# A first MLP product in seven block products instead of eight: w1's combinations kept in DRAM and fetched through a ring

## The chip, the cores and the metric

The kernel runs on one core of a Trainium2 chip. The metric is the device time of one execution in microseconds (us); the times given are medians of several runs. Lower is better.

## What is computed

The reference is one transformer-like block on x of 2048 positions by 512 channels, with a condition vector c that makes six modulation vectors. The first half is a spectral filter (a two-dimensional real FFT, a product with weights, the inverse FFT), the second half a dense MLP with the Mish activation:

```python
mod = (silu(c) @ w_mod).reshape(...)          # sa, ca, ga, sb, cb, gb
h = layernorm(x) * (1 + ca) + sa
x = x + ga * irfft2(rfft2(h) * (w_r + 1j * w_i))
h = layernorm(x) * (1 + cb) + sb
act = mish(h @ w1 + b1)                       # w1: 512 x 1376
x = x + gb * (act @ w2)                       # w2: 1376 x 512
```

Everything is float32. The change concerns `h @ w1`, and what has to be prepared for it.

## The kernel before

The x tile stays on the chip as 16 row blocks of 128 positions. The spectral half has three stages; the last of them, called p3 here, runs over the 16 row blocks in steps s = 0 to 16: `p3_col` (L707, L708) multiplies on TensorE into a bank of tag A, ScalarE copies the bank out (L710), `p3_row` (L717) multiplies the copy into a bank of tag B, and VectorE adds that to x (L720). `norm_sums` (L122, L123) then makes the row block's mean and variance for the second layer norm, and `norm_scale` (L127, L135, L147) turns these into scales.

The MLP works on eight blocks b of 256 positions (NB = 8) and on six groups t of features (NT = 6): t = 1 to 5 are pairs of feature tiles of 128, t = 0 is the last tile of 96. Float32 precision comes from splitting each operand into a high part (rounded to the fp32r format) and a low part (the rest), and adding three of the four products: high x high, high x low, low x high.

For one block, the channel dimension lies in four tiles k of 128. `transpose_in` (L686) and `split_in` (L694 to L699) bring a block's h into the tile h2, high and low parts beside each other, so that one matmul with w1's high part has 512 columns (L796) and one with w1's low part 256 (L798). `up` does four and four of them for each feature tile. `front` evicts: ScalarE moves the low half with the bias (L806), VectorE adds the high half (L807). `back` applies Mish (L813) and forms four sums of quarter tiles (L823) for the second product; `halves` splits these into high and low (L758, L759); `down` (L849, and L841 for t = 0) is the second product, which has seven block products over halves of positions, features and channels already. In the last block, t = 3, 4, 5 and 0 are done plainly by `last_down` (L862, L865). `gather`, `chain` and `residual` (L872 to L896) combine the seven results and add them to x, on VectorE.

w1 is loaded in twelve pieces during p3 (`load_w1`), copied to a high part on ScalarE (`split_w1`, L661) and subtracted to a low part on GpSimd (L662); both parts then stay on the chip. w2's pieces are loaded, summed on GpSimd (`sum_w2`, L755) and split (L758, L759) in p3 and in the first two blocks; gating and plain splits for the last block come late (L778). `mod_column` (L115) makes modulation sums on VectorE.

All engines run their own instructions in program order, and that order is written out by hand: a loop over s for p3, then a loop over the 48 items (b, t), each of which calls `up(s)`, `front(s)`, `halves(s - 1)`, `back(s)` and `down(s - LAG)` with LAG = 2, so that TensorE alternates one item's first product with the second product of the item two before.

## Time and profile before

| what | value |
|---|---|
| median of 3 runs | 382.56 us (381.71 to 382.67) |
| span of the profiled execution, first to last instruction | 380.1 us |
| busy: TensorE, its weight loads, VectorE, ScalarE, GpSimd | 373.7, 340.0, 300.2, 250.5, 99.1 us |
| data moved | 36.49 MB read from and 4.20 MB written to HBM |

The profiled execution has a span, which leaves out what lies before its first and after its last instruction; no time of its own is given beside that, and the median of the runs is 2.46 us above it. Engines are named PE (TensorE matmuls), PEld (its weight loads), DVE (VectorE), ACT (ScalarE), POOL (GpSimd) and SP (the queue that issues most transfers). A row such as "252.09 2.52 PE bank L849 x21" has the start and length in us, the engine, the tile written, the line of the kernel and the number of instructions. In a group row, the figure after the bar is busy time in us, then the mean length of one instruction in ns, then the engine's idle time before the group and what ended it.

### The profile page before, as it was taken

Reading aid. Unit: us, or ns where it says so; the run is one execution under the profiler, and the core shown is the slowest. Engines: PE = TensorE matmul, PEld = TensorE weight load, DVE = VectorE, ACT = ScalarE, POOL = GpSimd, SP = SyncE. Lnnn points to the kernel's source line nnn. Section 1 sums busy time; section 2 is a strip of 40 time slices with the busy share of each in tenths; the row PEclk is TensorE's granted clock in tenths of the full one; section 3 lists DMA queues with packets and bytes.
Section 4 is the critical chain, followed back from the end, with each engine's and each line's share of the span. In section 5 each row is a group of like instructions: output and inputs, shape, how many; then the busy total and the mean of one; then the engine's idle time right before and its main releaser. Section 6 shows DMA issues by size and latency. Waiting matters only on the chain.

```text
span 380.1 us, 7142 instructions
## 1 busy us (share of the span) xinstructions
PE 373.7 (98%) x2612; PEld 340.0 (89%) x2612; DVE 300.2 (79%) x688; ACT 250.5 (66%) x532; POOL 99.1 (26%) x134
## 2 busy tenths in 40 slices
PE   8999999998999999999999999999999999999996
PEld 8999967778999989998998998998998999899985
DVE  2898968886989989989749758757865976887994
ACT  1798789995497558865844845845765674685751
POOL 0588747883664611300000000000000010017000
PEclk9999999999999999999999999999999999999999
DMA  7999997776454221111000100100100200222011
GB/s 235 380 354 344 362 359 237 252 231 212 128 140 143 77 85 58 56 30 55 3 0 2 55 2 0 58 0 3 55 2 0 78 0 2 75 67 82 2 55 55
DMA packets 21746, 41.14 MB, mean 108 GB/s; under 512 B 4016, under 2 KB 7184, under 8 KB 21456
## 3 DMA queue, kind: packets, MB, share of 16 engines
q1 hardware_dynamic: 19552, 33.75, 26.3%
q10 hardware_dynamic: 2160, 6.95, 6.2%
q8 instruction: 20, 0.33, 0.3%
q14 instruction: 14, 0.11, 0.1%
HBM read 36.49 MB, written 4.20 MB: 107 GB/s over the span
## 4 chain that ended last, share of the span: by engine, by line
PE 93%; DVE 3%; ACT 1%; DMA 1%; issue 0%; SPq 0%; ACTq 0%
PE bank L849 24%; PE bank L796 21%; PE bank L798 10%; PE bank L707 4%; PE bank L717 4%; PE bank L708 4%; PE bank L498 4%; PE bank L208 4%; PE bank L547 3%; PE bank L253 3%; PE bank L841 2%; PE bank L862 2%; PE bank L478 2%; PE bank L686 2%; PE bank L255 1%; PE bank L254 1%
## 5 line engine op out<-in xcount | busy, mean ns | idle before, releaser
L806 ACT ACTIVATE buf<-bank,b1n 128x256 f32<-128x256 f32 (+1 forms) x88 | 40.8, 471 | 66.8 <-PE bank L798 64.2
L807 DVE TENSOR_TENSOR buf<-buf,bank 128x256 f32<-128x256 f32 (+1 forms) x88 | 35.4, 417 | 37.3 <-ACT buf L806 37.2
L759 DVE TENSOR_TENSOR al<-buf,ah 128x512 fp32r<-128x512 f32 (+2 forms) x85 | 52.9, 645 | 0.9 <-ACT ah L758 0.9
L778 POOL TENSOR_TENSOR buf<-buf,modr 128x512 f32<-128x512 f32 (+1 forms) x3 | 4.0, 1322 | 182.8 <-DMA buf<-in_B_w_dram 175.6
L796 PE MATMUL bank<-h2e,w1h 128*128 128x512 f32 (+1 forms) x176 | 48.4, 397 | 0.0
L796 PE MATMUL bank<-h2o,w1h 128*128 128x512 f32 (+1 forms) x176 | 48.3, 396 | 0.0
L758 ACT CAST ah<-buf 128x512 fp32r<-128x512 f32 (+2 forms) x85 | 43.0, 548 | 1.4 <-DVE buf L823 1.1
L823 DVE TENSOR_TENSOR buf<-buf 128x128 f32<-128x128 f32 x148 | 40.8, 317 | 3.5 <-ACT buf L813 2.2
L813 ACT ACTIVATE buf<-buf 128x512 f32<-128x512 f32 (+1 forms) x48 | 28.6, 596 | 14.8 <-DVE buf L807 14.7
L849 PE MATMUL bank<-w2a,ah 128*128 128x256 f32 x161 | 34.9, 286 | 0.0
L796 PEld LDWEIGHTS bank<-h2e,w1h 128*128 128x128 f32 (+1 forms) x176 | 30.1, 187 | 4.5
L796 PEld LDWEIGHTS bank<-h2o,w1h 128*128 128x128 f32 (+1 forms) x176 | 30.1, 187 | 4.4
L849 PE MATMUL bank<-w2b,ah 128*128 128x256 f32 x147 | 31.8, 283 | 0.0
L798 PEld LDWEIGHTS bank<-h2o,w1l 128*128 128x128 f32 (+1 forms) x176 | 26.7, 185 | 4.2
L798 PEld LDWEIGHTS bank<-h2e,w1l 128*128 128x128 f32 (+1 forms) x176 | 26.7, 185 | 4.1
L798 PE MATMUL bank<-h2o,w1l 128*128 128x256 f32 (+1 forms) x176 | 27.8, 280 | 0.0
L798 PE MATMUL bank<-h2e,w1l 128*128 128x256 f32 (+1 forms) x176 | 27.8, 279 | 0.0
L849 PEld LDWEIGHTS bank<-w2a,ah 128*128 128x128 f32 x161 | 26.7, 191 | 0.0
L707 PE MATMUL bank<-kc,d 128*128 128x128 f32 x128 | 24.8, 276 | 0.5 <-ACT d L391 0.5
L708 PE MATMUL bank<-kc,d 128*128 128x128 f32 x128 | 24.7, 275 | 0.0
L849 PEld LDWEIGHTS bank<-w2b,ah 128*128 128x128 f32 x147 | 24.6, 191 | 0.0
L122 DVE BATCH_NORM_STATS2 st<-x 128x6 f32<-128x512 f32 x32 | 22.0, 689 | 0.4
(228 smaller groups left out, 981.1 us busy)
## 6 DMA issues: line engine op xcount, KB each, us to landing
buf<-in_B_w_dram SPq DMA_DIRECT2D x20, 256.0 KB, 3.0
x<-in_A_x_dram SPq DMA_DIRECT2D x16, 256.0 KB, 4.9
xring<-in_x_t_dram SPq DMA_DIRECT2D x16, 256.0 KB, 4.7
out_dram<-x SPq DMA_DIRECT2D x7, 512.0 KB, 2.6
buf<-in_w_mod_dram SPq DMA_DIRECT2D x9, 256.0 KB, 3.1
mraw<-in_km_dram SPq DMA_DIRECT2D x16, 128.0 KB, 4.7
wqa<-in_w_q_dram SPq DMA_DIRECT2D x4, 512.0 KB, 6.8
wqb<-in_w_q_dram SPq DMA_DIRECT2D x4, 512.0 KB, 7.2
```

The costliest lines, as they stand in the source:

```text
L122: nc.vector.bn_stats(t, x[:, n, :])
L707: nc.tensor.matmul(o, dj[:, 0:128], kc[0][:, n, :], start=True, stop=False)
L708: nc.tensor.matmul(o, dj[:, 64:192], kc[1][:, n, :], start=False, stop=True)
L758: nc.scalar.copy(h, r)
L759: nc.vector.tensor_tensor(l, r, plain(h), op=ALU.subtract)
L796: nc.tensor.matmul(ps, w1h[:, k, fs], h[:, k], start=(k == 0), stop=False)
L798: nc.tensor.matmul(ps[:, 0:256], w1l[:, k, fs], h[:, k, 0], start=False, stop=(k == 3))
L806: nc.scalar.activation(o, ps[:, 256:], AF.Identity, bias=b1n[:rows, f:f + 1])
L807: nc.vector.tensor_tensor(o, o, ps[:, 0:256], op=ALU.add)
L813: nc.scalar.activation(o, o, AF.Mish)
L823: nc.vector.tensor_tensor(o, p, q, op=op)
L849: nc.tensor.matmul(o, a[p][:, e], w2[t][q][:, r], start=(own and half == 0 and t == 1 and i == 0), stop=(end and i == 2 and (n, half) != ( ...
```

## The change

The first product is done over pairs: i counts four pairs of neighbouring blocks (s0 = 2i, s1 = 2i + 1), t = 1 to 5 the pairs of feature tiles, and the 512 channels are two halves. In each (i, t), w1's part is a 2 x 2 arrangement A11, A12, A21, A22 (features by channels) and h a 2 x 2 arrangement B11, B12, B21, B22 (channels by positions). The eight products of the parts become seven, by sums of parts (Winograd's form of Strassen's scheme): S1 = A21 + A22, S2 = S1 - A11, S3 = A11 - A21, S4 = A12 - S2; T1 = B12 - B11, T2 = B22 - T1, T3 = B22 - B12, T4 = B21 - T2. Each of the seven products has six matmuls of 256 columns: two channel tiles, three terms of high and low parts.

- The operands of w1 (three parts and four sums for each t, 256 KB each with high and low parts) are made once, written to DRAM (`keep_w1`), and in later pairs of blocks fetched (`fetch_w1`) into a ring of eight slots. Those of t = 2, 3 and 1 are made in p3, those of t = 4 and 5 during the first pair of blocks. The sums (`sum_w1`) are formed on GpSimd; the low part is a subtraction on VectorE for A11, A12 and A22 and on GpSimd for the sums.
- h is scaled into raw buffers (`scale_in`), T1 to T4 are formed on GpSimd (`sum_in`), and all eight arrangements are split by ScalarE and VectorE (`split_in`).
- The products of one (i, t) accumulate in one bank of tag A (two halves) and half a bank of tag D. The half named x[0:256] takes products 1, 6, 7 and 4 in turn; `evict` reads it after each with ScalarE. VectorE adds after products 2, 7 and 3.
- The single tile t = 0 is done without the scheme, in matmuls of 256 columns (`up_single`), and its second product is also cut to 256 columns.
- The residual's products and additions move from VectorE to GpSimd, in pieces of 512.
- The loop over items is gone. Every call gets a key, and the calls are issued in the order of their keys: one key is one of the seven products, and between two of them two pieces of three matmuls of the second product are issued. In the first pair of blocks only block 0's second products run beside the first products; from then on two blocks' run for each pair, and the last block's run after all first products.
- The scratch memory for descriptors is cut from 8192 to 1024 bytes.

The core of the diff:

```diff
-LAG = 2
+PRODUCTS = {1: ("A11", "B11"), 2: ("A12", "B21"), 3: ("S4", "B22"), 4: ("A22", "T4"), 5: ("S1", "T1"),
+            6: ("S2", "T2"), 7: ("S3", "T3")}
...
-    w1h = pm.tile([P, 4, F], F32R, name="w1h")
-    w1l = pm.tile([P, 4, F], F32R, name="w1l")
...
+    kept = {(t, a): dram.tile([P, 512], F32, name=f"w1_{t}_{a}") for t in range(1, NT) for a, _ in PRODUCTS.values()}
...
+    def space(t, a, k):
+        if (t, a) in ring:
+            return
+        w = act.tile([P, 7, P], F32R, name=("ah", "al")[k % 2]).rearrange("p e s -> p (e s)")
+        ring[t, a] = w[:, 0:512].rearrange("p (i k f) -> p i k f", i=2, k=2)
+
+    def slot_w1(key):
+        ring[key] = pm.tile([P, 2, 2, P], F32R, name="wr", tag="wr", bufs=8)
+
+    def fetch_w1(t, a):
+        slot_w1((t, a))
+        nc.sync.dma_start(plain(ring[t, a].rearrange("p i k f -> p (i k f)")), kept[t, a])
+
+    def sum_w1(t, a):
+        p, q, op = {"S1": ("A21", "A22", ALU.add), "S2": ("S1", "A11", ALU.subtract),
+                    "S3": ("A11", "A21", ALU.subtract), "S4": ("A12", "S2", ALU.subtract)}[a]
...
+        nc.gpsimd.tensor_tensor(src[t, a], src[t, p], src[t, q], op=op)
+
+    def split_w1(t, a):
+        w = ring[t, a]
+        nc.scalar.copy(w[:, 0], src[t, a])
+        eng = nc.vector if a[0] == "A" else nc.gpsimd
+        eng.tensor_tensor(w[:, 1], src[t, a], plain(w[:, 0]), op=ALU.subtract)
+
+    def keep_w1(t, a):
+        w = ring[t, a] if t > 3 or t == 1 and (t, a) in near else ring.pop((t, a))
+        nc.sync.dma_start(kept[t, a], plain(w.rearrange("p i k f -> p (i k f)")))
...
+    def sum_in(b, dst=None):
+        p, q = {"T1": ("B12", "B11"), "T2": ("B22", "T1"), "T3": ("B22", "B12"), "T4": ("B21", "T2")}[b]
...
+        nc.gpsimd.tensor_tensor(raws[b], p, q, op=ALU.subtract)
...
-            for k in range(4):
-                nc.tensor.matmul(ps, w1h[:, k, fs], h[:, k], start=(k == 0), stop=False)
-            for k in range(4):
-                nc.tensor.matmul(ps[:, 0:256], w1l[:, k, fs], h[:, k, 0], start=False, stop=(k == 3))
...
+    def up(i, t, j):
+        a, b = PRODUCTS[j]
+        w, h = ring.pop((t, a)), slots[b]
+        o = region(i, t, j)
+        n = 0
+        for p, q in TERMS:
+            for k in range(2):
+                nc.tensor.matmul(o, w[:, p, k, :], h[:, q, k, :], start=(j in (1, 5) and n == 0), stop=(n == 5),
+                                 skip_group_check=True)
+                n += 1
...
+        if j == 1:
+            identity(hold(s0, t)[:, 0:256], ps, f)
+        if j == 6:
+            identity(hold(s1, t)[:, 0:256], ps, f)
+        if j == 2:
+            o = raw[s0, t][:, 0:256]
+            nc.vector.tensor_tensor(o, o, ps, op=ALU.add)
+        if j == 7:
+            o = raw[s1, t][:, 256:]
+            identity(o, ps, f + 1)
+            nc.vector.tensor_tensor(o, o, ups[i, t, "z"][:, 0:256], op=ALU.add)
+        if j == 4:
+            nc.scalar.activation(raw[s0, t][:, 256:], ps, AF.Mish, bias=b1n[:, f + 1:f + 2])
+            o = raw[s0, t][:, 0:256]
+            nc.scalar.activation(o, o, AF.Mish)
+        if j == 3:
+            o = raw[s1, t][:, 0:256]
+            nc.vector.tensor_tensor(o, o, ps, op=ALU.add)
...
-        nc.vector.tensor_tensor(rows, rows, gbr.unsqueeze(1).to_broadcast([P, 2, D]), op=ALU.mult)
+        for i, r in enumerate((r0, r1)):
+            xb = x[:, 2 * b + i, :]
+            nc.gpsimd.tensor_tensor(r, r, gbr, op=ALU.mult)
+            nc.gpsimd.tensor_tensor(xb, xb, r, op=ALU.add)
...
+    def plan_w1(plan, t, load, key, step, at):
+        k = 7 * (t - 2)
+        plan.at(load, load_w1, t, at)
+        for i, a in enumerate(("A11", "S1", "A12", "S2", "A22", "S4", "S3")):
+            now = key + step * i
+            plan.at(now, space, t, a, k + i)
+            if a[0] == "S":
+                plan.at(now + 0.01, sum_w1, t, a)
+            late = now + 0.02 if a[0] == "A" else now + 3.4 * step
+            plan.at(late, split_w1, t, a)
+            plan.at(late + 0.55 * step, keep_w1, t, a)
...
+    plan_w1(plan, 2, 0.7, 2.1, 0.5, 0)
+    plan_w1(plan, 3, 2.5, 5.7, 0.5, 2)
...
+    plan_w1(plan, 1, 6.5, 9.3, 0.5, 0)
...
+    for b, s, dst in (("T1", 12, "B11"), ("T2", 12, None), ("T3", 13, None), ("T4", 13, "B21")):
+        plan.at(s + 0.5, sum_in, b, dst)
+    for b, s in (("B11", 11), ("B21", 12), ("T2", 14), ("T1", 14.5), ("T3", 15), ("T4", 16)):
+        plan.at(s + 0.4, split_in, b)
...
+            units += [(i, t, 1)] + [prev + (j,) for j in (4, 3)] + [(i, t, j) for j in (6, 2, 5, 7)]
...
+        if i == 0 and t > 3:
+            plan.at(k - 7.9, slot_w1, (t, a))
+            plan.at(k - (7.5 if t == 4 else 4.7), split_w1, t, a)
+            plan.at(k - 3, keep_w1, t, a)
+        elif k >= 8:
+            plan.at(k - 7.9, fetch_w1, t, a)
...
+            plan.at(key - 3.2, sums, b, t)
+            lead = 1.9 if t == 4 else 2.4
+            plan.at(key - lead, halves, b, t, 0)
+            plan.at(key - lead + 0.7, halves, b, t, 1)
...
+            for c in range(n):
+                plan.at(key + 0.5 * c, down, b, t, c)
```

532 lines of the change are left out of this document (301 added, 231 removed).

## The prediction

> **What bounds the kernel now.** I read the page's head first, then the windows by stage, then the chain of waits that ended last, and last single rows. The page gives the span, the busy time of each engine, and the chain that ended last by engine:
>
> ```profile
> span 380.1 us, 7142 instructions
> PE 373.7 (98%) x2612; PEld 340.0 (89%) x2612; DVE 300.2 (79%) x688; ACT 250.5 (66%) x532; POOL 99.1 (26%) x134
> PE 93%; DVE 3%; ACT 1%; DMA 1%; issue 0%; SPq 0%; ACTq 0%
> ```
>
> TensorE is the bound on average; whether it is where the change works is for the windows to say (a stretch in us and its length; busy us and instructions of PE, PEld, DVE, ACT and POOL; granted clock, DMA share, GB/s):
>
> ```profile
> 92.00:136.00 44.00, 44.00 (x388) 43.58 (x388) 38.95 (x78) 27.05 (x55) 23.78 (x24) 1.00 0.42 121
> 136.00:172.00 36.00, 35.92 (x239) 32.46 (x238) 33.72 (x80) 26.68 (x55) 6.79 (x8) 1.00 0.21 60
> 172.00:232.50 60.50, 60.50 (x415) 55.85 (x414) 43.21 (x104) 37.19 (x77) 0.00 (x0) 1.00 0.05 18
> ```
>
> The first row is the last stage of the spectral part (p3), in which the MLP's weights are prepared; the second is the MLP's start, the third two of its blocks in the steady state. TensorE has no gap in any of them, at full granted clock. In the steady state VectorE is 71% busy, ScalarE 61%, GpSimd idle and DMA at 5%: there is room for what the change adds. In p3 VectorE is at 89% and GpSimd at 54%, and then VectorE is at 94%: little room. So the gain is read from the third row, the danger from the first two.
>
> **What TensorE saves.** The chain gives the issue price of each shape (start, us, line, matmuls):
>
> ```profile
> 171.88 1.38 PE bank L841 x6
> 252.09 2.52 PE bank L849 x21
> 254.61 0.93 PE bank L796 x4
> 255.54 0.47 PE bank L798 x4
> 256.01 0.94 PE bank L796 x4
> ```
>
> L796 is the 512-column product with w1's high part, L798 the 256-column one with its low part: a feature tile of one block costs 0.93 + 0.47 = 1.40 us, two tiles of two blocks 5.60 us. L849 is the second product, whose matmuls are 256 columns wide, as all the new ones are: 2.52 / 21 = 0.12 us. The change does seven products of six matmuls, 42 x 0.12 = 5.04 us: 0.56 us less for each of 20 pairs (five pairs of tiles, four of blocks), 11.2 us. By L798's 0.47 / 4 = 0.1175 us it would be 5.60 - 4.94 = 0.66 us, 13.3 us in all. I take 0.12, since the new groups of six alternate with groups of three of L849's kind. The Trainium skill ("TensorE: Matmul & The Clock Gate", section "Wait — 56ns, not 53.3ns?") has a warm matmul start every N / 2.4 GHz + 2.5 ns, so 109 ns and 216 ns; this trace has 117.5 to 120 ns and 232 ns, and by the page's figures the estimate would be 12.2 us.
>
> The number of weight loads goes from 32 to 42 per pair. Their row (ns min/median/max, first and last start):
>
> ```profile
> L849 PEld LDWEIGHTS bank<-w2a,ah x161: 187/192/192, 151.7 to 362.3; 128*128 128x128 f32 x161
> ```
>
> A load of 192 ns stands before every 0.12 us matmul of L849 and is already in its interval, so I add nothing. The pairs would break even at 5.60 / 42 = 0.133 us for a matmul.
>
> Two pieces get dearer. The second product of the single 96-row tile goes from six wide matmuls (L841, 1.38 us) to twelve narrow ones, 1.44 us: 7 x 0.06 = 0.4 us. Its first product becomes twelve narrow ones, 1.44 for 1.41 us: 0.2 us. TensorE's own time falls by 11.2 - 0.6 = 10.6 us. Transposes stay, and blocks 0 to 7 keep the other matmuls of the second product.
>
> **What the change puts on VectorE and GpSimd.** Prices without company are from the steady state, where GpSimd is idle (busy us, mean ns):
>
> ```profile
> L823 DVE TENSOR_TENSOR buf<-buf 128x128 f32<-128x128 f32 x40 | 9.8, 287 | 1.1 <-ACT buf L813 0.7
> L807 DVE TENSOR_TENSOR buf<-buf,bank 128x256 f32<-128x256 f32 x20 | 8.2, 418 | 10.6 <-ACT buf L806 10.6
> L759 DVE TENSOR_TENSOR al<-buf,ah 128x512 fp32r<-128x512 f32 x10 | 6.9, 691 | 0.0
> L759 DVE TENSOR_TENSOR al<-buf,ah 128x384 fp32r<-128x384 f32 x10 | 5.6, 557 | 0.0
> ```
>
> Beside GpSimd the same operation is longer. From p3, groups and then single starts:
>
> ```profile
> L699 DVE TENSOR_TENSOR h2e<-buf,h2e 128x512 fp32r<-128x512 f32 x2 | 2.2, 1102 | 0.0
> L759 DVE TENSOR_TENSOR w2a<-buf,w2a 128x512 fp32r<-128x512 f32 x1 | 1.8, 1766 | 0.0
> L759 DVE TENSOR_TENSOR w2a<-buf,w2hi 128x512 fp32r<-128x512 f32 x1 | 1.8, 1761 | 0.0
> L759 DVE TENSOR_TENSOR w<-buf,w 128x512 fp32r<-128x512 f32 x1 | 1.2, 1218 | 0.0
> L759 DVE TENSOR_TENSOR w2a<-buf,w2a 128x256 fp32r<-128x256 f32 x1 | 0.4, 406 | 0.0
> L759 DVE TENSOR_TENSOR w2a<-modr,w2a 128x1024 fp32r<-128x1024 f32 x1 | 1.2, 1193 | 0.0
> L115 DVE SCALAR_TENSOR_TENSOR buf<-buf,bank 128x512 f32<-128x512 f32 x3 | 2.0, 672 | 1.4 <-DMA buf<-in_w_mod_dram 1.4
> L135 DVE SCALAR_TENSOR_TENSOR ve<-ve,rstd 128x2 f32<-128x2 f32 x2 | 1.6, 818 | 0.1
> L135 DVE SCALAR_TENSOR_TENSOR ve<-ve,rstd 128x4 f32<-128x4 f32 x2 | 0.3, 161 | 0.1
> L720 DVE TENSOR_TENSOR x<-x,bank 128x512 f32<-128x512 f32 x16 | 10.8, 675 | 2.4 <-PE bank L717 2.1
> ```
>
> ```profile
> 110.01 0.73 POOL L755 TENSOR_TENSOR modr<-buf 128x256 f32<-128x256 f32 x1
> 117.57 2.09 DVE L759 TENSOR_TENSOR w2a<-buf,w2a 128x256 fp32r<-128x256 f32 x2
> 117.70 1.42 POOL L662 TENSOR_TENSOR w1l<-buf,w1h 128x512 fp32r<-128x512 f32 x1 [2.13 <-ACT w1h L661]
> 122.83 1.28 POOL L662 TENSOR_TENSOR w1l<-buf,w1h 128x512 fp32r<-128x512 f32 x1 [1.76 <-ACT w1h L661]
> ```
>
> The pair at 117.57 needs about 0.41 + 0.69 us alone, and took 2.09, because its second half did not end before GpSimd's operation had. Operations of VectorE that read PSUM (L720) are not stretched. The five stretched subtractions lost (1766 + 1761 + 1218 - 3 x 691) + 2 x (1102 - 691) ns = 3.5 us, and the two of L135 at 818 ns against 161 another 1.3 us: some 5 us of p3's 38.95.
>
> In p3 the change replaces GpSimd's twelve low parts of w1 by 12 sums and 12 low parts of combinations (24 x 0.73 = 17.5 us), keeps 12 sums for w2 (8.8 us), and adds four sums of h (4 x 1.28 = 5.1 us) and the single tile's low part, about 1 us: 32.4 us against 23.78. VectorE gets nine low parts of w1 (9 x 0.41 = 3.7 us) and six splits of h in place of two (4 x 0.69 = 2.8 us). If the stretch grows with the number of its SBUF operations (13 more beside some 28, a factor of 1.4) and with GpSimd's time (32.4 / 23.78, again 1.4), 5 us becomes about 10 us, and VectorE has 38.95 + 6.5 + 5 = 50.5 us to do in 44. How late may it be before TensorE waits?
>
> ```profile
> 93.72 1.06 PE L717 MATMUL bank<-kiv,buf 128*128 128x128 f32 x8
> 94.61 0.39 PE L707 MATMUL bank<-kc,d 128*128 128x128 f32 x2
> 96.40 1.06 PE L717 MATMUL bank<-kiv,buf 128*128 128x128 f32 x8
> ```
>
> A step is 2.68 us, and L717's products go to two banks, so an addition (L720) may end up to 5.36 - 1.06 = 4.3 us after its products; it takes 0.68, so 3.6 us of lateness cost nothing. That leaves 50.5 - 44 - 3.6 = 2.9 us. The bounds: nothing, if TensorE's first MLP units (which need only B11 and w1's first combination) are reached with VectorE late, as it may be there; and, if VectorE and GpSimd never work beside each other on SBUF, 32.4 us of GpSimd and 16 us of VectorE (3.7, six splits at 0.69, the w2 splits' 5.7 from 406, 691 and 1193 ns, 16 small ones at 0.16) in the 13 steps that have them, 48.4 - 34.8 = 13.6, less 3.6: 10 us.
>
> ScalarE's queue has its own hazard there. w1's combinations of the later tiles are written into four slots that are read by the transfer to DRAM, and for two of them a tile, twice, the reading transfer is issued only a fraction of a step before the next write. Transfers of 256 KB land after 3.0 us:
>
> ```profile
> buf<-in_B_w_dram SPq DMA_DIRECT2D x20, 256.0 KB, 3.0
> ```
>
> The waiting copy holds up L710's eviction behind it, for which TensorE waits once it is over 1.2 us late (a step of 2.68 less the 0.89 us between the starts of L717 and the next column product, less 0.59 for the copy): 0 to 1.4 us each, four times, 0 to 5.6 us. It passes while VectorE is late anyway, and I take 1 us beyond the 2.9: p3 costs 3.9 us, between 0 and 10.
>
> In the first pair of blocks, evictions (15 x 0.42), sums and splits of one block's activations (5 x (9.8 + 6.9 + 5.6) / 10 + 0.4), w1's last splits (6 x 0.41), w2's (2 x 2.3 and 1.9), eight splits of h (8 x 0.69), four gate sums (4 x 0.75 with their read), the block's end (2 x 0.69 + 2 x 0.42) and small ones (0.6) make some 38 us of VectorE for some 43 us of TensorE (35 groups of 0.72, the single tile's 2.9 and one block's second product, 5 x 2.52 + 1.44, are 42.1; the transposes come on top), with 29 us of GpSimd beside it (24 x 0.73 for w1 and w2, 5.1 for the sums of h, 2 x 0.73 + 4 x 1.28 for the residual). By the rate of p3 that stretches VectorE by 5 to 8 us: just full. I take 1 us, between 0 and 7.
>
> In the steady state, a pair of blocks has 5 evictions by VectorE fewer (2.1 us) and both residuals moved to GpSimd, against four more splits of h (2.8 us); GpSimd gets about 18 us of 57. VectorE has room, and waits of at most 1.28 us are covered by parts issued two to three keys ahead (a key, one product of 0.72 us and two groups of 0.36, is 1.44 us). I take 0.1 us for each of three pairs, between 0 and 4 us in all.
>
> The ring: 35 fetches of 256 KB a pair of blocks, each issued on SP about eight products ahead, some 10 us, against 3.0 us to land. The stores behind them on SP wait for a slot at most, and nobody waits for these. At 9 MB in 57 us that is 157 GB/s, and the DMA share of 5% has the room. I cost it at nothing; without that lead each fetch would cost up to 3 us.
>
> The sum against the profiled execution: 380.1 - 10.6 + 3.9 + 1 + 0.3 = 374.7 us of span; the median of the runs, 382.56, lies 2.46 us above the span, so 377.2 us, and I say 377. A difference of 0.3%, 1.1 us, is about what a measurement here can tell from none.
>
> **Rivals.**
>
> All is hidden: TensorE stays without a gap, 382.56 - 10.6 = 372 us, or 370 by 0.1175. For it: the third window. Against it: VectorE at 94% after p3.
>
> VectorE and GpSimd become the bound until the second pair of blocks. For it: the stretched rows, and that both queues get more just there. It decides from the point where the last sum of h ends after p3's last product, since VectorE's queue then stands at the split of that sum with p3's last additions behind it. Price: 10 us in p3; in the first pair 29 us of GpSimd and 26 of VectorE's SBUF operations (the sums and splits above) in 43, less the 6.6 us residual that may slip, 5.4; and 1 us in each later pair: 382.56 - 10.6 + 10 + 5.4 + 3 = 390 us. The Trainium skill ("SBUF — State Buffer", section "SBUF: two separate sides") states it as a rule: a VectorE operation with two SBUF inputs and a GpSimd operation that reads SBUF exclude each other. By that rule the trace agrees at 117.57. Against it as the outcome: work in both queues is only due at its user.
>
> Halves of a bank: one 256-column region takes products 1, 6, 7 and 4 in turn, and each waits until ScalarE has read the one before. Between 7 and 4 lies one product and two or three groups of L849, 1.4 us; early in the first pair one product, 0.72 us. The eviction:
>
> ```profile
> L806 ACT ACTIVATE buf<-bank,b1n 128x256 f32<-128x256 f32 x20 | 9.4, 472 | 15.9 <-PE bank L798 15.9
> ```
>
> 0.47 us fits, unless ScalarE's queue stands at a copy that waits for VectorE. With a quarter of a microsecond for each of 20 pairs' tight waits it gives 377 + 5 = 382 us, no change.
>
> The change could also not save what it says, if a narrow matmul of the new order took over 0.133 us: at 0.14 it adds 42 x 0.14 - 5.60 = 0.28 us to each of 20 pairs, and with the other costs it is 382.56 + 5.6 + 0.6 + 5.2 = 394 us. The 21 in a row of L849 speak against it.
>
> **How the numbers follow.** Forecast (374 to 381) 0.45; all hidden 0.15; the shared bound 0.28; narrow matmuls too dear 0.02; halves of a bank 0.10, half of it no change and half slower. So faster 0.60, the same 0.05, slower 0.35. The range goes from 370.5, the hidden case, to 391, past the 390 of the second rival. The forecast's own range is 374 to 381.
>
> **What would show it.** Right: steady windows with TensorE full and a pair of blocks in some 57.7 us for 60.5; gaps of a few us at p3's end, put down to VectorE's additions (L720's successor) or ScalarE's copies; rows of the new products at 0.12 us. Wrong: a matmul interval over 0.13 us; gaps of 10 us or more in p3 and after with GpSimd full; waits of TensorE on ScalarE's evictions all along the steady state; or products that wait for a fetch.

## The result: 442.4 us, 15.6% slower

The changed kernel took 442.44 us (median; the kernel before beside it 382.58 us): a ratio of 1.156, 95% interval 1.152 to 1.160. The forecast was 377, the range 370.5 to 391, and the likeliest sign was the wrong one. The profiled execution took 443.01 us, with a span of 441.0.

First the page of the changed kernel: its span, the engines' busy time, the granted clock in 40 slices, and the chain that ended last by engine.

```profile
span 441.0 us, 8229 instructions
PE 392.6 (89%) x2886; PEld 368.3 (84%) x2886; DVE 333.1 (76%) x659; ACT 255.9 (58%) x560; POOL 203.1 (46%) x227
...
PEclk9999999999998878996989999988999999999969
...
PE 50%; DVE 33%; ACT 7%; DMA 4%; issue 4%; POOL 1%; SPq 1%; DVEq 0%; ACTq 0%; POOLq 0%
```

Before, TensorE held 93% of the chain and VectorE 3%. Now VectorE holds a third of it, although it is busy for no larger share of the span than before (76% for 79%): it is not full, it is late at particular places. And the row of granted clocks, all nines before, has sixes, sevens and eights from the thirteenth slice on.

The same windows by stage (stretch and length; busy us and instructions of PE, PEld, DVE, ACT, POOL; clock, DMA share, GB/s): p3, the first pair of blocks, the next pair, the end.

```profile
92.00:142.00 50.00, 45.02 (x388) 44.00 (x386) 44.92 (x81) 33.00 (x74) 35.26 (x41) 0.98 0.63 212
142.00:218.00 76.00, 60.36 (x407) 57.68 (x406) 50.05 (x103) 43.65 (x95) 26.69 (x29) 0.86 0.57 181
218.00:285.00 67.00, 62.17 (x496) 61.00 (x495) 49.40 (x95) 38.09 (x81) 20.66 (x16) 0.97 0.52 157
...
411.00:441.00 30.00, 19.32 (x105) 16.19 (x104) 23.14 (x28) 7.57 (x15) 16.60 (x13) 0.87 0.10 36
```

In the first pair nobody is full: TensorE 79%, VectorE 66%, ScalarE 57%, GpSimd 35%. What TensorE waited for (us in total, times, longest):

```profile
PE bank L940 <- DVE al L792: 16.5, 13, 3.7
PE bank L845 <- DVE even L862: 8.7, 4, 3.5
PE bank L845 <- DVE scb L862: 5.4, 2, 4.2
PE bank L754 <- DVE x L757: 2.7, 1, 2.7
```

L940 is the second product, which waits for the low parts of the activations (`halves`, L792). L845 is a first product that waits for VectorE's addition after product 2 (`evict`, L862), because that frees its half of a bank. No row names a fetch of the ring.

For a balance I took from both traces the time from each matmul's start to the next, less what is usual for its shape (the 20th percentile). Excess over 0.3 us at once is a gap; the rest is a slowed matmul, nearly all of it at half clock.

| stage (us of the changed kernel) | gaps | slowed | gaps and slowed before |
|---|---|---|---|
| p3, 92 to 142 | 5.6 | 2.2 | 0.4 |
| first pair, 142 to 218 | 17.3 | 10.6 | 0.9 |
| 218 to 411, the other pairs | 16.3 | 10.1 | 2.4 |
| end, 411 to 441 | 8.3 | 3.4 | 0.2 |
| sum | 47.5 | 26.3 | 3.9 |

That is 69.9 us more; the matmuls' usual intervals sum to 271.9 us for 280.8, so 8.9 us less. The difference, 61.0 us, is the change of the span (60.9). TensorE's saving is there; nearly eight times as much is lost beside it. The split is good to about 2 us: with the 20th percentile of each shape over the whole span as the usual interval, the saving comes to 7.1 us and the loss to 68.1.

Where the steady loss comes from shows in VectorE's, GpSimd's and TensorE's own rows of one place (start, length in us):

```profile
286.99 3.59 DVE L910 TENSOR_TENSOR buf<-buf 128x128 f32<-128x128 f32 x4
290.50 3.30 DVE L792 TENSOR_TENSOR al<-buf,ah 128x384 fp32r<-128x384 f32 x2
293.72 0.41 DVE L862 TENSOR_TENSOR even<-even,bank 128x256 f32<-128x256 f32 x1
294.06 1.01 DVE L910 TENSOR_TENSOR buf<-buf 128x128 f32<-128x128 f32 x4
...
287.64 1.29 POOL L989 TENSOR_TENSOR modr<-modr 128x512 f32<-128x512 f32 x1
289.01 1.41 POOL L990 TENSOR_TENSOR x<-x,modr 128x512 f32<-128x512 f32 x1
290.39 1.31 POOL L989 TENSOR_TENSOR modr<-modr 128x512 f32<-128x512 f32 x1
291.78 1.47 POOL L990 TENSOR_TENSOR x<-x,modr 128x512 f32<-128x512 f32 x1
...
289.08 0.88 PE L845 MATMUL bank<-hT,wr 128*128 128x256 f32 x6
292.17 0.39 PE L940 MATMUL bank<-w2a,al 128*128 128x256 f32 x1 [1.97 <-DVE al L792]
294.19 1.65 PE L845 MATMUL bank<-hT,wr 128*128 128x256 f32 x6 [1.27 <-DVE even L862]
```

Four sums of 128 columns on VectorE take 1.0 us when GpSimd is idle, as at 294.06. The four before them take 3.59: GpSimd runs the residual's four large operations back to back, and three of VectorE's four end only behind an operation of GpSimd (one gets through in 0.28 us). The two splits behind them (0.56 and 0.69 us alone) take 3.30, each held up once more, and the addition that frees the bank stands behind those. TensorE waits 1.97 and 1.27 us. The Trainium skill ("SBUF — State Buffer", section "SBUF: two separate sides") has a VectorE operation with two SBUF inputs and a GpSimd operation that reads SBUF exclude each other for the whole instruction; the row of 3.59 us agrees. Behind the wait the six matmuls take 1.65 us for 0.88: the clock is halved.

### The profile page after: what moved, and what is told of

Same layout as the page of the kernel before. It is cut to its first block, busy times and chain, and to the rows that moved or that the text cites. A ratio compares the mean times of both kernels' runs of the same rounds, so it can differ in the third digit from the quotient of the medians.

```text
span 441.0 us, 8229 instructions
## 1 busy us (share of the span) xinstructions
PE 392.6 (89%) x2886; PEld 368.3 (84%) x2886; DVE 333.1 (76%) x659; ACT 255.9 (58%) x560; POOL 203.1 (46%) x227
## 4 chain that ended last, share of the span: by engine, by line
PE 50%; DVE 33%; ACT 7%; DMA 4%; issue 4%; POOL 1%; SPq 1%; DVEq 0%; ACTq 0%; POOLq 0%
PE bank L845 14%; PE bank L940 11%; DVE buf L910 10%; DVE al L792 7%; PE bank L500 3%; PE bank L210 3%; PE bank L549 2%; PE bank L255 2%; DVE w2a L792 2%; PE bank L480 2%; DVE hB L736 2%; DMA w_S<-al 2%; DVE st L124 1%; ACT ah L791 1%; PE bank L952 1%
## 5 line engine op out<-in xcount | busy, mean ns | idle before, releaser
L845 PE MATMUL bank<-hT,wr 128*128 128x256 f32 x480 | 76.3, 299 | 15.5 <-DVE even L862 8.7
L845 PEld LDWEIGHTS bank<-hT,wr 128*128 128x128 f32 x480 | 67.8, 206 | 17.2 <-DVE even L862 9.5
L791 ACT CAST ah<-buf 128x512 fp32r<-128x512 f32 (+1 forms) x45 | 27.0, 603 | 42.0 <-DVE buf L910 38.4
L792 DVE TENSOR_TENSOR al<-buf,ah 128x512 fp32r<-128x512 f32 (+1 forms) x45 | 42.8, 957 | 8.9 <-ACT ah L791 8.5
L845 PE MATMUL bank<-hB,wr 128*128 128x256 f32 x240 | 40.8, 313 | 1.8 <-ACT odd L850 1.7
L940 PE MATMUL bank<-w2a,ah 128*128 128x256 f32 x161 | 39.5, 309 | 0.0
L845 PEld LDWEIGHTS bank<-hB,wr 128*128 128x128 f32 x240 | 35.6, 216 | 3.6 <-ACT odd L850 2.9
L940 PE MATMUL bank<-w2b,ah 128*128 128x256 f32 x147 | 33.8, 291 | 0.0
L940 PEld LDWEIGHTS bank<-w2a,ah 128*128 128x128 f32 x161 | 30.5, 219 | 0.0
L940 PE MATMUL bank<-w2a,al 128*128 128x256 f32 x56 | 18.8, 336 | 10.8 <-DVE al L792 10.8
L850 ACT ACTIVATE odd<-bank,b1n 128x256 f32<-128x256 f32 x25 | 11.8, 474 | 27.4 <-PE bank L845 27.3
L940 PEld LDWEIGHTS bank<-w2b,ah 128*128 128x128 f32 x147 | 25.6, 199 | 0.0
L940 PE MATMUL bank<-w,ah 128*128 128x256 f32 x112 | 22.9, 296 | 0.6 <-DVE modr L978 0.5
L940 PEld LDWEIGHTS bank<-w2a,al 128*128 128x128 f32 x56 | 12.9, 231 | 12.6 <-DVE al L792 12.6
L731 POOL TENSOR_TENSOR buf<-buf 128x512 f32<-128x512 f32 x13 | 18.2, 1411 | 9.5 <-DVE hB L736 8.1
L990 POOL TENSOR_TENSOR x<-x,modr 128x512 f32<-128x512 f32 x14 | 21.0, 1501 | 1.1
L255 PE MATMUL bank<-buf,mring 128*128 128x512 f32 x48 | 20.6, 430 | 0.2 <-DVE buf L248 0.2
```

Of the source, the lines that this page charges most:

```text
L255: nc.tensor.matmul(pa, m[:, a, 0:128], g, start=(i == 0), stop=False)
L731: nc.gpsimd.tensor_tensor(raws[b], p, q, op=ALU.subtract)
L791: nc.scalar.copy(h, r)
L792: nc.vector.tensor_tensor(l, r, plain(h), op=ALU.subtract)
L845: nc.tensor.matmul(o, w[:, p, k, :], h[:, q, k, :], start=(j in (1, 5) and n == 0), stop=(n == 5), skip_group_check=True)
L940: nc.tensor.matmul(out_ps[b][n][:, 256 * half:256 * half + 256], a[p][:, e], w2[t][q][:, r], start=(t == 1 and half == 0 and i == 0), stop ...
```

## The experiments

All were compared with the kernel before on the same chip; its medians there lie between 382.1 and 382.4 us, so the runs can be compared with one another too. "Gaps" and "slowed" are worked out as in the table.

**1 to 4: is it the residual and h's sums on GpSimd?** e1 puts the residual back on VectorE where it stood, e2 the four sums of h, e3 both; e4 is the reverse, the kernel before with its residual on GpSimd.

```diff
 def residual(b):              # e1, e3: six operations (e4: the reverse)
-    nc.gpsimd.tensor_tensor(...)
+    nc.vector.tensor_tensor(...)
 def sum_in(b, dst=None):      # e2, e3
-    nc.gpsimd.tensor_tensor(raws[b], p, q, op=ALU.subtract)
+    nc.vector.tensor_tensor(raws[b], p, q, op=ALU.subtract)
```

> The changed kernel with the residual's six operations a block put back on VectorE (in pieces of 512), all else as changed. Shared-port theory: VectorE's activation sums (L910) and splits (L792) wait for GpSimd's residual operations, TensorE waits for them, and the clock halves after the gap. Then the gaps of 2.1 and 1.4 us per pair of blocks (224, 290, 357 us) go, with the half-clock stretches behind them and part of the 8 us of gaps in the last 30 us: 422 to 432 us. Rival (it is the order of the waits: bank halves, evictions and the ring, not who computes): VectorE gets some 3.6 us more for each block and the time stays or rises: 440 to 455 us.

> The changed kernel with the four sums of h for each pair of blocks (T1 to T4) formed on VectorE in place of GpSimd, all else as changed. Shared-port theory: each is 0.69 us on VectorE against 1.3 to 1.4 us on GpSimd with VectorE blocked meanwhile; the gap of 1.5 us per pair at 272 and 339 us goes and p3's end gets a few us better: 430 to 438 us. Rival (VectorE has too much to do in p3 and the first pair of blocks): 442 to 450 us.

> Both of the former: residual and sums of h on VectorE; GpSimd keeps only w1's and w2's sums and low parts. Shared-port theory: the gains add, TensorE has no gap over 0.5 us in the second to fourth pair of blocks, and what stays is p3 and the first pair: 412 to 425 us. Rival: at or above the changed kernel's 442 us.

> The kernel before with one part of the change alone: its residual on GpSimd in pieces of 512, six operations a block. Shared-port theory: VectorE's sums and splits are stretched by 3 to 6 us a block, seen in their mean; TensorE's look-ahead of two items (some 10 us) covers part of it: 384 to 398 us, with gaps at the residuals if above. Rival (the stretch is harmless, what hurts is the new order): 382 to 384 us without a gap in TensorE.

Measured: e1 434.56 us, ratio 1.137 (1.131 to 1.142); e2 436.99, 1.142 (1.137 to 1.147); e3 432.44, 1.127 (1.119 to 1.135); e4 387.68, 1.014 (1.010 to 1.018). e2 and e4 lie in what was expected; e1 and e3 gave far less than the theory of the shared port wanted. In e3 nothing runs on GpSimd in the steady pairs, and a gap of 2.4 us a pair remains. Its chain there (start, length, what):

```profile
284.14 0.70 DVE modr L989
...
284.86 0.69 DVE x L990
285.56 0.61 DVE modr L989
...
286.19 0.69 DVE x L990
286.88 0.60 DVE al L792
287.48 0.34 DVE even L862
...
287.87 1.55 PE bank L845 x6
```

The same six operations, now at VectorE's own pace, stand in a lump ahead of a split and of the addition that TensorE needs; the product behind runs at half clock again. And in e4 GpSimd's six operations also come in a lump, and VectorE's sums and splits are stretched by 3.7 us a block, as expected; yet its steady blocks have no gap and take 30.6 us for 30.3, since VectorE's queue has slack there. Only the last block has a gap, of 2.5 us, with 3.4 us of half clock behind it. So the port alone is not the cause, nor is a lump wherever it stands: the loss comes where a lump holds up VectorE just ahead of what TensorE needs next.

**5: spread the lump.** From e3, the residual's six operations get keys of their own, about one key apart, each just behind an eviction.

```diff
-        plan.at(at + 1.6, residual, b)
+        for res_part, late in enumerate((2.1, 2.6, 3.1, 4.1, 5.1, 6.1)):
+            plan.at(int(at) + late if b < NB - 1 else at + late - 0.5, residual, b, res_part)
```

> Residual and sums of h on VectorE as in the run before it with both, and the residual's six operations no longer in one lump before the next products' evictions but one key apart, each behind the eviction of its key. Theory (VectorE's queue order decides in the steady state; TensorE waits for the eviction after product 2, which stood behind the lump): the gap of 2.4 us for each pair of blocks goes, with the half-clock stretch behind it, some 5 us for each of three pairs and 2 to 4 us at the end: 412 to 420 us, and a pair of blocks takes 57 to 59 us. Rival (other waits take its place): 425 to 432 us.

Measured: 414.23 us, 1.083 (1.081 to 1.086), as its theory expected: 18 us less than e3, by order alone. The window of a steady pair, and from the timeline one product's six matmuls and what follows:

```profile
215.00:273.00 58.00, 58.00 (x483) 57.79 (x483) 44.79 (x109) 36.63 (x78) 0.00 (x0) 1.00 0.62 176
```

```profile
252.75 0.88 PE L845 MATMUL bank<-hT,wr 128*128 128x256 f32 x6
253.47 0.40 PE L940 MATMUL bank<-w2a,ah 128*128 128x256 f32 x2
```

TensorE has no gap, at full clock, and a pair of blocks takes 58.3 us (`gather` of block 0 at 215.2, of block 2 at 273.5) for 60.6 before. The six matmuls take 253.47 - 252.75 = 0.72 us, 0.12 each. 28 of the 60 us are gone: 10 with the two kinds of work back on VectorE (e3), 18 with the lump spread. e5 is the base of most runs below. What is left lies in p3, the first pair and the end.

**6: is it the clock?** Matmuls that nobody reads are put into four of the first pair's waits (56 calls).

```diff
+        if (i, t, j) in ((0, 1, 6), (0, 2, 5)):
+            plan.at(k - 0.1, warm, 16 if j == 6 else 8, "C")
+        if (i, t, j) in ((0, 3, 7), (0, 5, 7)):
+            plan.at(k - 0.1, warm_in, i, t)
         plan.at(k, up, i, t, j)
```

> The spread kernel with 56 small matmuls added whose results nobody reads, in front of four places of the first pair of blocks at which TensorE waits (16 before product 6 of the first tiles, 8 before product 5 of the second, 16 each before product 7 of the third and fifth). They are some 6 us of TensorE time if nothing hides them. Theory (the granted clock halves because TensorE has just stood still): half-clock time in p3 and the first pair falls from 14 to 20 us to under 8, and the time is 3 to 8 us below the spread kernel's. Rival (the clock does not follow the gaps): the same half-clock time, and 2 to 6 us above it.

Measured: 414.02 us, 1.082 (1.076 to 1.088): no gain. The half-clock time in the first pair fell from 13.7 to 6.2 us and the gaps from 15.2 to 6.7, but the added matmuls took 12.2 us, twice the 6 expected (the 56 calls are 112 matmuls in the trace). The clock follows the standstills; filling them with idle work only moves the time.

**7: leave out the sums.** e5 without w1's sums and h's.

> The spread kernel without the sums: w1's four combinations of each tile pair and h's four sums are left out, and an operand takes the place of each (splits, transfers and products stay). It shows what the sums cost in p3 and the first pair. Theory (sums on GpSimd and VectorE, and their exclusion on SBUF, fill p3 and the first pair): 8 to 15 us below the spread kernel's, with less lateness of VectorE at p3's end. Rival (splits, evictions and the queue's order alone suffice for the loss): within 4 us of it.

Measured: 402.58 us, 1.053 (1.050 to 1.056): 11.7 us less, as the first theory expected, and 20 us over the kernel before remain.

**8: is the narrow matmul right?** The kernel before, with 42 narrow matmuls for a pair of tiles in two blocks.

> The kernel before, with the first product of tile pairs 1 to 5 in 42 matmuls of 256 columns for two tiles and two blocks in place of 16 of 512 and 16 of 256 (the last one or two products of w1's low part are left out for each tile). It is TensorE's saving alone, with none of the change's other work. If the sum over TensorE is right (42 x 0.12 for 5.60 us, 20 times): 371 to 373 us. If narrow matmuls with a weight load each cost more than 0.12 us: 376 us and more.

Measured: 374.37 us, 0.980 (0.977 to 0.983). From its chain:

```profile
241.27 2.49 PE bank L799 x21
```

2.49 / 21 = 0.119 us: the narrow matmul costs what the prediction took. A pair of blocks takes 58.0 us and the time falls by nearly 8, a little less than the 371 to 373 us expected, with gaps of 2.6 us in all. This is also the one kernel here below the kernel before, and it is no version of the change: it shows what seven products could bring if their operands cost nothing.

**9: order in the first pair.** From e5, whatever stood on VectorE less than 0.9 of a key ahead of an eviction goes behind it.

```diff
+    for n, (key, order_no, fn, args) in enumerate(plan):
+        if fn in (split_w1, split_w2, sums, halves, split_in, sum_in, residual, low_w2, gate_sum):
+            for k in behind:          # keys of products 2 and 3 in the first pair
+                if k - 0.9 < key < k + 0.05:
+                    plan[n] = k + 0.06, order_no, fn, args
```

> The run before, with the residual spread on VectorE, and one more rule for the order of VectorE's queue in the first pair of blocks: a split, sum or gate operation that stood less than 0.9 of a key ahead of the eviction after product 2 or 3 now stands right behind it. Nothing is taken out. If the first pair stands still because evictions queue behind work that is not yet due, its gaps (15.2 us, in 11 places) fall to 6 to 10 us, the half-clock stretches with them, and the time falls by 5 to 12 us against 414.2, to 402 to 409. If VectorE and GpSimd simply have too much to do there, the gaps come back at the moved operations' own users and the time stays within 3 us of 414.2.

Measured: 413.71 us, 1.081 (1.079 to 1.084): nothing. The gaps in the first pair came to 14.9 us for 15.2. Some were shorter, others new, probably because what was moved was itself due soon after; the longest entry among TensorE's waits is now for ScalarE's evictions (L850, 4.9 us, five times).

**10 and 12: the lump or the port?** Both have the residual on GpSimd. e10 is the change with e5's six keys and nothing else; e12 is e5 with the six on GpSimd, each behind a small operation that reads what VectorE's last eviction wrote.

```diff
+        fresh = st["fresh"]           # e12: four columns of VectorE's last eviction
+        nc.gpsimd.tensor_tensor(tie, fresh, fresh, op=ALU.add)
```

> The change itself, with one thing altered: the residual's six operations stand one key apart, each behind an eviction, and they stay on GpSimd, as h's sums do. Only an order is changed. If the steady gaps of the change (2.15 + 1.44 + 1.5 us a pair) come from six operations in a lump that VectorE's queue then meets, the two from the residual go, and the third (from h's sums) stays: gaps of 1.5 to 2 us a pair, the time 421 to 429. If GpSimd's operations cost as much wherever they stand, because each holds up an operation of VectorE by its own length, gaps of about the same sum come in other places, and the time stays at 436 to 444. If the order is all, GpSimd included, the time is that of the run with the residual spread on VectorE, 412 to 420.

> The run with the residual spread on VectorE, with the same six operations at the same keys, but on GpSimd, and each behind a four-column GpSimd operation that reads what VectorE's last eviction wrote, so that GpSimd cannot run them back to back. If the harm of the residual on GpSimd is that it meets VectorE's lump of small operations (each then as long as one GpSimd operation), spreading helps here as it did on VectorE: 412 to 420, no gap in the steady pairs. If GpSimd's operations hold up VectorE by their own length wherever they stand, six of 1.3 to 1.4 us a block stay as 8 us of VectorE's time in 29: pairs of 60 us or more with gaps, 422 to 440.

Measured: e10 442.38 us, 1.159 (1.155 to 1.164); e12 419.52, 1.098 (1.096 to 1.100). e10's edit did not do what it was written for: GpSimd has nothing else in its queue there, so whatever the keys, it starts each operation as soon as the one before is done, and its rows stand back to back as before. That is no evidence for the port. e12 is: from its VectorE and GpSimd rows,

```profile
218.86 1.60 DVE L913 TENSOR_TENSOR buf<-buf 128x128 f32<-128x128 f32 x4
222.85 1.38 DVE L913 TENSOR_TENSOR buf<-odd 128x128 f32<-128x128 f32 x1
224.69 1.31 DVE L793 TENSOR_TENSOR al<-odd,ah 128x384 fp32r<-128x384 f32 x1
...
222.70 1.39 POOL L998 TENSOR_TENSOR modr<-modr 128x512 f32<-128x512 f32 x1
224.25 1.34 POOL L1000 TENSOR_TENSOR x<-x,modr 128x512 f32<-128x512 f32 x1
```

each GpSimd operation still holds up one of VectorE's (1.38 us for 0.28, 1.31 for 0.56), but with an eviction in between no two add up on the same wait, and a pair takes 58.9 us on average (`gather` of block 0 at 215.4, of block 4 at 333.2). Set beside the other runs with h's sums on VectorE, it parts the lump from the port (time, and a pair of blocks on average):

| residual | on VectorE | on GpSimd |
|---|---|---|
| in a lump | e3: 432.44 us, a pair 62.6 | e2: 436.99 us, a pair 65.3 |
| spread | e5: 414.23 us, a pair 58.3 | e12: 419.52 us, a pair 58.9 |

Spreading is worth 18.2 us on VectorE and 17.5 on GpSimd; the place is worth 4.6 us in the lump and 5.3 spread (e12's six small operations a block included). So the lump is the larger part and the port the smaller: the port costs 0.6 us a pair when the work is spread and 2.7 in the lump, the lump 4.3 us a pair on VectorE alone. With h's sums on GpSimd as well, as in the change, a pair takes 66.3 us (from 217.8 and 350.5). Of e12's 5 us over e5, 4 come after 333 us, where it has two gaps of 3.9 us.

**11: a late load?** In e5, a chain through four queues stood in the first pair: the load of w1's last half, which waits for its buffer; GpSimd's sum; ScalarE's copy of it; VectorE's subtraction.

```profile
186.43 0.38 SPq L662 DMA_DIRECT2D odd<-in_B_w_dram  x1
189.59 0.74 POOL L686 TENSOR_TENSOR wsum<-odd,odd 128x256 f32<-128x256 f32 x1 [0.93 <-DMA odd<-in_B_w_dram]
191.17 0.41 ACT L690 CAST wr<-wsum 128x256 fp32r<-128x256 f32 x1 [3.74 <-POOL wsum L686]
192.79 0.58 DVE L692 TENSOR_TENSOR wr<-odd,wr 128x256 fp32r<-128x256 f32 x1 [4.73 <-ACT wr L690]
```

> The run with the residual spread on VectorE, without one of its 128-row loads of w1: the second half of the last pair of feature tiles is not loaded in the first pair of blocks, and what the buffer still holds from the pair before is used (so this tile's combinations hold other data; no operation of an engine is left out). In that run the load is issued at 186.4 us because its buffer is then still read, GpSimd's sum starts when it lands at 189.6, ScalarE's queue stands 3.7 us for the sum and VectorE's 4.7 us for ScalarE's copy. If such waits of one in-order queue for the next are what fills the first pair, the gap of 2.8 us at 197.6 and the half-clock time behind it go: the time falls by 3 to 8 us, to 406 to 411. If the engines' own loads set the first pair's length, it stays within 2 us of 414.2.

Measured: 413.33 us, 1.082 (1.080 to 1.085): within 2 us, so this theory falls. Without the load:

```profile
187.52 0.41 ACT L691 CAST wr<-wsum 128x256 fp32r<-128x256 f32 x1 [2.77 <-POOL wsum L687]
190.11 0.43 DVE L693 TENSOR_TENSOR wr<-odd,wr 128x256 fp32r<-128x256 f32 x1 [4.72 <-ACT wr L691]
...
197.83 0.98 PE L846 MATMUL bank<-hT,wr 128*128 128x256 f32 x6 [2.65 <-DVE scb L863]
```

VectorE still idles 4.72 us. ScalarE still waits 2.77 us for GpSimd's sum, since GpSimd's queue had itself stood for a copy of ScalarE's, and after that ScalarE comes to an eviction that waits for TensorE before it comes to VectorE's copy. Then VectorE has the delayed work in a rush, and TensorE waits 2.65 us. The load was only the last of several things that ended together.

**13 to 16: take out a part of the preparation, and all three.** e13: no work on w1 in the first pair (finished combinations of other tiles are fetched). e14: no last preparation of w2. e15: no sums and splits of h's sums in p3. e16: all three.

```diff
-            plan.at(k - 7.9, slot_w1, (t, a))                             # e13
-            plan.at(k - (7.5 if t == 4 else 4.7), split_w1, t, a)
+            plan.at(k - 7.9, ready_w1, t, a)       # fetch kept[t - 2, a]
...
-            gate_w2(t)                                                    # e14, and plain_w2's splits
...
-    for b, s, dst in (("T1", 12, "B11"), ("T2", 12, None), ...): ...      # e15, and four split_in
```

> The run with the residual spread on VectorE, without the work on w1 in the first pair of blocks: the combinations of the last two pairs of feature tiles are not summed, copied and split there (8 sums and 8 low parts by GpSimd, 14 copies by ScalarE, 6 low parts by VectorE); each is instead fetched from DRAM, where those of two tile pairs before stand, and stored again as before (so these tiles use other weights). p3 stays as it is. If this preparation is what the first pair lacks room for, its standstills and slowed matmuls there (15.2 + 8.2 us) fall to under 10 us and the time by 10 to 18 us, to 396 to 404. If what is late there comes out of p3, or is h's own preparation, the time stays within 4 us of 414.2.

> The run with the residual spread on VectorE, without the last preparation of w2: GpSimd's gate products on the five reloaded tiles of w2 and the six splits of ScalarE and VectorE (12 operations of 512 columns) are left out, and the last block uses what the buffers hold (so its output is other). If they hold up VectorE in the last two blocks, the standstills and slowed matmuls there (4.3 + 2.3 + 2.4 + 2.3 us from 332 us on) fall to under 4 us and the time by 6 to 10 us, to 404 to 408. If the activations of two blocks at once are what VectorE is late with, it stays within 3 us of 414.2.

> The run with the residual spread on VectorE, without the four sums of h's blocks and their four splits in p3 (8 operations of 512 columns on VectorE, 4 copies on ScalarE); the first pair's products with these sums read a plain block instead, so its values are others. Where the first pair is late with what p3 leaves in VectorE's queue, p3's last gaps (2.0 and 2.3 us), the one before the first evictions (2.5) and the half-clock time after it go: the time falls by 8 to 16 us, to 398 to 406. If p3's backlog is absorbed anyway, it stays within 3 us of 414.2.

> The three omissions together: no work on w1 in the first pair, no last preparation of w2, no sums and splits of h's sums in p3 (their times alone: 409.9, 406.0 and that of the run beside this one). If they are what the remaining standstills come from and simply add up, the sum is 414.2 - 4.3 - 8.2 - 8 to 16, that is 386 to 394, with under 10 us of standstills after 92 us. If one hides behind another, it stays over 396; if the standstills breed each other by the clock, it is under 386.

Measured: e13 409.94 us, 1.073 (1.070 to 1.076); e14 405.97, 1.062 (1.060 to 1.063); e15 408.97, 1.068 (1.065 to 1.072); e16 396.88, 1.037 (1.034 to 1.040). Against e5's 414.2 that is 4.3, 8.3 and 5.3 us. e14 came out as its first theory expected (standstills and slowed matmuls after 332 us fell from 11.3 to 4.4). e13 and e15 fell between their theories: each is a part of the first pair's loss, neither is its cause. e16 is 17.4 us below e5, and the three alone sum to 17.9: they add up. It missed its expected 386 to 394 because e15's part was smaller than expected; 396.88 is where the second theory put it (over 396), but not because one hides behind another. Its gaps after 92 us came to 18.0 us, not to under 10.

In e16 the first pair (142 to 205 us) still has gaps of 10.0 us and 6.2 of slowed matmuls, with VectorE at 61%. Two of its waits, the second the longest, with the rows of ScalarE and VectorE that they wait for:

```profile
150.86 0.98 PE L850 MATMUL bank<-hB,wr 128*128 128x256 f32 x6 [1.34 <-ACT buf L855]
167.63 1.59 PE L850 MATMUL bank<-hB,wr 128*128 128x256 f32 x6 [2.36 <-DVE even L867]
...
147.45 1.28 ACT L873 ACT_TABLE_LOAD   x1 [1.12 <-PE bank L850]
148.74 0.47 ACT L873 ACTIVATE even<-bank,b1n 128x256 f32<-128x256 f32 x1
149.42 0.60 ACT L795 CAST w2b<-buf 96x512 fp32r<-96x512 f32 x1
149.93 0.51 ACT L795 CAST ah<-even 128x384 fp32r<-128x384 f32 x1
150.34 0.47 ACT L855 ACTIVATE buf<-bank,b1n 128x256 f32<-128x256 f32 x1
...
164.48 1.04 ACT L795 CAST w2b<-modr 128x1024 fp32r<-128x1024 f32 x1
165.55 1.22 DVE L796 TENSOR_TENSOR w2b<-modr,w2b 128x1024 fp32r<-128x1024 f32 x1 [1.93 <-ACT w2b L795]
167.16 0.41 DVE L867 TENSOR_TENSOR even<-even,bank 128x256 f32<-128x256 f32 x1
```

The product at 150.86 needs its half of a bank, which ScalarE reads at 150.34. In ScalarE's queue stand ahead of that the loading of the activation table (1.28 us), the two activations of product 4 and two copies. The product at 167.63 waits for VectorE's addition after product 2 (L867). Ahead of that stands a split of w2 in 1024 columns, for whose copy VectorE sits idle 1.93 us, since the copy itself stands late in ScalarE's queue. The same wait, 2.67 us long, stands in the change at 174.36 and in e5 at 175.60: no run leaves that split out. Nothing there is long, and no engine is full, but one product takes TensorE 0.72 us and each of these queues is some 3 us long. How much of e16's first pair each such place costs stays open: no experiment moved them one by one.

## Why the prediction was wrong, point by point

**TensorE's saving (10.6 us): right in kind, a little large.** Reckoned for a steady pair: 5 x 0.56 less the dearer single tile, a pair in some 57.7 us. Measured in e5: 58.3 for 60.6; in e8: 58.0; over the whole change 7 to 9 us. The narrow matmul takes 0.12 us. (The prediction's side estimate of 12.2 us works out as 12.3 by the formula quoted there; nothing hangs on it.) The rival "not save what it says" is out, and so is a fault of the ring: no wait of TensorE on a fetch.

**p3 (3.9 us, between 0 and 10): in its bounds, too small.** Measured 7.8 us, gaps 5.6 and slowed 2.2. The mechanisms named were the right ones: TensorE waits 2.7 us for an addition of VectorE (L757), where 2.9 were reckoned, and ScalarE waited 2.6 us in all for the reading transfers of the combinations' slots (taken as 1). The largest part that a run prices is h's sums and splits at the end of p3: with what follows from them in the first pair, e15 puts them at 5.3 us (with the sums on VectorE, as in e5).

**The first pair (1 us, between 0 and 7): the step that failed most.** Measured 27.9 us. The working compared sums: 38 us of VectorE against 43 of TensorE, "just full". VectorE's load was too small in it: it was busy for 50.05 us, against 38 and 5 to 8 of stretch, and TensorE's matmuls at their usual intervals need 48.1. But VectorE was never full there (50.05 of 76 us); it waited and then was late. In p3 an addition may be 3.6 us late; a product of the first pair needs a read of its half of a bank one unit or so later. The chain at its first gap, in the changed kernel:

```profile
145.97 0.61 DVE x L757
...
147.44 0.14 DVE hT L736
...
148.01 0.42 DVE even L862
148.48 1.57 PE bank L845 x11
```

The lateness that p3 had absorbed (its last addition, its last statistics and h's splits) stands in VectorE's queue ahead of L862, and TensorE stops for 3.5 us. "Halves of a bank" was named among the rivals, at a quarter of a microsecond for each of 20 pairs; it had the condition right (0.47 us fits "unless ScalarE's queue stands at a copy"), the reader for the largest waits wrong (VectorE after product 2) and the place wrong (the first pair, not all along).

**The steady state (0.3 us, between 0 and 4): failed.** Measured 26.4 us, gaps 16.3 and slowed 10.1. The step was "waits of at most 1.28 us are covered by parts issued two to three keys ahead". One wait is; here four 512-column operations of GpSimd come back to back, most of VectorE's that stand beside them are held up by one each, and the lead of 2.4 keys was used up by the lump. A lump on VectorE itself does it too (e3). e5 and e12 bring the gaps of the steady pairs to 0 and 0.4 us a pair.

**The end: no term at all.** Measured 11.7 us, gaps 8.3 and slowed 3.4. The plan does both blocks' first products before the last second products, so the last preparation of w2 no longer has a first product beside it. e14 prices that preparation at 8.3 us.

**The clock: not considered.** Half-clock stretches sum to 44.4 us in the change (without a last one that begins with the span's last microsecond), and most of its 26.3 us of slowed matmuls lie in them. Every estimate priced a wait at its own length; in e3 a gap of 2.4 us brought 1.6 us of slowed matmuls, and a pair of blocks takes 62.6 us there for 58.3 in e5: the wait cost 1.7 times its length.

**The rival "VectorE and GpSimd become the bound until the second pair" (390 us)** had the sign and the first mechanism, with 1 us for each later pair where 8 were lost. It took a shared port to cost its overlap, once. Of the 60 us, 10 went with the residual and h's sums back on VectorE (e3), 18 with the residual's lump spread (e5), 8 with the last preparation of w2, 5 with h's sums in p3 and 4 with w1's work in the first pair; 14.5 are what remains in e16 over the kernel before, with TensorE's saving already taken off. What fills those is in part shown by rows, as above, and in part open.

## What to carry to other kernels

When work moves to an idle engine, look up where its operations will run back to back, and which short operations of the other engine stand beside that stretch: the price is set by the lump and by what is queued behind it, not by the sum of busy time. A new schedule's first and last stretches need a sum of their own, with each wait's lead in us beside it, since preparation has no cover there. And where TensorE's standstills sum to some 2 us within one clock window of 3.41 us, price them at their length plus half of the window behind it.

## What the runs showed of the hardware

- The clock is halved in stretches of 3.41 us or multiples of it, after standstills shorter than that. Its changes lie on a grid of 3.41 us (the half-clock starts 139.8, 150.1, 160.3 and 174.0 us in the change lie 3, 3 and 4 steps apart), and what counts is the sum of the gaps within one step of the grid, not the length of one gap. In all 18 traces, from 92 us to the last matmul, none of the 1440 full-clock steps with under 1.8 us of gaps (those over 0.3 us, as in the table) was followed by half clock, and all of the 67 with over 2.03 us were; in between it went either way. So a gap of 2.4 us in e3 (at 285.5) and one of 2.5 us in e4 were each followed by 3.41 us at half clock, and in e5 two gaps of 1.22 and 1.28 us in the step from 160.6 us were too; but a gap of 2.83 us in e5 (172.8 to 175.6), which falls as 1.51 and 1.32 us into two steps, was followed by none. The Trainium skill ("TensorE: Matmul & The Clock Gate", section "What's actually happening") has half rate after an idle window of about 3.4 us; the ratio and the length agree, but some 2 us of standstill within one window were enough here.
- A chain of short VectorE operations beside a busy GpSimd is not stretched by a factor: single operations of it end only behind one of GpSimd's and the others run at their own length. Three of four were held up in the change (3.59 us for four that take 1.0 alone).
- Keys order an engine's queue only against its own work. An engine with an empty queue starts when its data are there, and six operations given six keys ran back to back (e10).
